# Two small queue changes in a fused long-convolution and state-space kernel: the taps' load on ScalarE's queue, the last stores on SyncE's

## The chip, the cores and the metric

The kernel runs on one core of one Trainium2 chip. The metric is the device time of one execution in microseconds, lower being better. The kernel before took 378.06 us, the median of five runs (377.67 to 381.59).

## The reference, cut to what matters

Two heads work on sequences of 2048 rows and 1024 channels, and their outputs stand side by side in the result.

```python
# head A: a 4-tap convolution, a long convolution by FFT, and a gate
k_shift = sum of k_pad[:, t:t + S, :] * shift_k[:, 3 - t]      # t = 0..3
kv = k_shift * v
y  = irfft(rfft(kv, 2 * S) * rfft(ssm_k, 2 * S))[:S] + kv * ssm_D
a  = q * y
# head B: a diagonal complex recurrence between two projections
Bu = einsum("bld,pd->blp", x, B_bar)
h_t = Lam_bar * h_(t-1) + Bu_t
b  = 2 * real(einsum("blp,dp->bld", h, Cmat)) + x * Dskip
out = concatenate([a, b], axis=-1)
```

`shift_k` holds four taps for each of the 1024 channels, 8 KB in all.

## The kernel before, in words

**Head B** is cut into 16 chunks of 128 time steps. For a chunk, TensorE projects the transposed input (`U`, line 460), ScalarE casts the result out of PSUM (`ue`), VectorE rotates it, scans it along time and rotates it back (`r1`, `r2`, `rc`, `sc`, `r3`, `r4`), TensorE projects to the output (`y_`, lines 529 and 534), ScalarE casts (`ye`, line 545) and a DMA stores the chunk (`yst`, line 553). The last chunk, 15, is stored in two halves directly from `ye` (line 547), because `CFG['th']` names it.

**Head A** is a long convolution written as matrix products, in three stages with scratch tensors in HBM between them. `kvm`, `kv1`, `kv2` and `kva` apply the taps and multiply by v; `am` and `ae` transform, and `ast` (line 627) writes the result to the scratch tensor `Ys_kv`; a parallel path does the same for the filter. The middle stage multiplies spectra. In the last stage, over eight values of u, `a3` transforms back, `a3e` casts into a tile `ot`, `qm` (line 780) multiplies it by q, and `op` (line 786) stores it in four DMAs of 128 KB each.

**Taps.** `ld_w` loads `shift_k` as two rows of 4 KB, one DMA each (line 398). `wb` (line 410) is a matmul of a row of ones with 512 values of such a row, which copies the taps to all 128 partitions; eight of them are needed, the first four reading the second row. `wbe` (line 414) casts each out of PSUM into `wbc`.

**Order.** All of it is written out by hand in one list, `ORDER`, and each engine executes its own instructions in the order of that list. A queue is in order too: an engine that issues a DMA and has to wait for the data holds up everything behind it on that engine. The list begins with `ld_w`. On TensorE the first entries are 22 warm-up products (`wm`), the transposes of one weight block (`bT.6.1`), five more warm-up products, then `wb.4`; on ScalarE the first computing instruction is `bc.6.1` (line 435), a copy of that transposed block. The loads of head B (`bl`, line 429) and of k (`kp`, lines 560 to 562) open SyncE's queue.

The end of the list, with everything but the entries around the stores left out, reads:

```python
... qm.5 ... op.7 ... ye.14.0 ... op.4 ... qp.1 ... ye.14.1 ... op.5 ... qm.0 ... r4.15.1 qm.1 yst.14
y.15.0.2 y.15.0.3 y.15.1.2 ye.15.0 op.0 y.15.1.3 ye.15.1 op.1 yst.15
```

`qp.1` is the last load on SyncE's queue. `yst.15` issues nothing, since chunk 15 is stored by `ye`. Before the change, GpSimd issues every store but those two halves of chunk 15. At the end of the program, line 849 of the launch, the engines drain, and SyncE waits for the outstanding DMAs, before the final signals between engines.

Of the kernel before, what the change touches and what calls it, by code (L numbers as in the profile page):

```python
# [44 lines left out]
    return f(F1), f(F1h), f(G), f(W3)  # L45


CFG = {'kr': 8, 'bdve': 4, 'K4': 13, 'kq': 2, 'tabct': 0, 'swsp': 1, 'th': (15,), 'actsw': ()}

ORDER = """  # L50
ld_w:a0a1 bl.6.1:b0 bl.0.1:b1 kp.-2 ld_G ld_sd ld_F bl.2.1:b2 bl.0.0:b3 wm.22:p0 bT.6.1:p0 wm.5:p1 wb.4:p1 bc.6.1 wb.5:p2 bl.1.0:b4 wb.6:p3 wb.7:p4
# [99 lines left out]
def full_kernel(ctx, tc, A_q, A_k, A_v, A_shift_k, A_ssm_k, A_ssm_D, B_x, B_Lre, B_Lim, B_Bre, B_Bim,  # L151
                B_Cre, B_Cim, B_log_dt, B_Dskip, out, cfg=None):
    c = dict(CFG)
    c.update(cfg or {})
    nc = tc.nc
# [5 lines left out]
    T = 128  # L161
# [6 lines left out]
    out_b = out[0][:, D:2 * D]  # L168
    spd = nc.sync.dma_start
    gpd = nc.gpsimd.dma_start  # L170
# [34 lines left out]
    kr = k.rearrange("(n r s) d -> r n s d", n=32, r=4)  # L205
    vr = v.rearrange("(n r s) d -> r n s d", n=32, r=4)
    qr = q.rearrange("(n r s) d -> r n s d", n=32, r=4)
    oar = out_a.rearrange("(n r s) d -> r n s d", n=32, r=4)
# [9 lines left out]
    st, pools, cms = {}, {}, {}  # L218
# [23 lines left out]
    def k4(name, shape):  # L242
        return rtile(ring, "a", name, shape)
# [143 lines left out]
    def taps_home():  # L387
        if "wbc" not in st:
            a1 = ap_pool("a1")
            st["wbc"] = a1.tile([P, 4, D], BF16, name="wbc", bufs=1)  # L390
            st["kring"] = a1.tile([P, c["kr"], D], BF16, name="kring", bufs=1)
            nc.vector.memset(st["kring"][0:1, 0:4, :], 0.0)

    def ld_w():
        taps_home()
        st["wraw"] = [k4("hk", [P, S]) for _ in range(2)]
        for m in range(2):
            gpd(st["wraw"][m][0:1, :], A_shift_k.rearrange("(o d) j -> o (d j)", o=2)[m:m + 1, :])
    E["ld_w"] = ld_w
    E["ld_F"] = lambda: (gpd(F1t[:], F1d.ap()), gpd(Fht[:].rearrange("p c k -> p (c k)"), Fhd.ap()))  # L400
    E["ld_G"] = lambda: gpd(Gt[:], Gd.ap())
# [148 lines left out]
    def yst(i):  # L550
        yo = st.pop(("yo", i))
        if i not in c["th"]:
            gpd(out_b[i * T:(i + 1) * T, :], yo[:])
    E["yst"] = yst

    def kp(r):
# [225 lines left out]

    def op(u):
        t_ = st.pop(("ot", u))
        for b in range(4):
            gpd(oar[b, :, 2 * u:2 * u + 2, :], t_[32 * b:32 * b + 32, :, :])
    E["op"] = op

    with tc.manual_schedule():
# [64 lines left out]
```

## Time and profile before

| what | value |
|---|---|
| median of five runs | 378.06 us |
| the profiled execution, its own time | 378.51 us |
| its span | 376.6 us |
| TensorE busy | 356.3 us (95%) |
| VectorE busy | 324.8 us (86%) |
| ScalarE busy | 278.3 us (74%) |
| GpSimd busy | 71.7 us (19%) |
| DMA, hardware queue of SyncE | 66.3% of 16 engines' span |
| DMA, software queue of GpSimd | 26.2% |
| line 398, the taps' two DMAs, issue to landing | 4.6 us |
| line 786, stores of `ot`, issue to landing in the last 17 us (median) | 2.7 us |
| line 547, stores of chunk 15, issue to landing | 3.0 us |

The span runs from the first to the last event that the profile records; the 1.9 us that the run's own time has beyond it lies around the program. TensorE is the busiest engine, but a share of the whole says nothing of the first microseconds or the last, and the change touches only these. They have to be read from the timeline, which lists instructions by their start.

### The profile page before, as it was taken

The page shows a single profiled execution, that of the slowest core. Times are in us where ns is not written, and L with a number is a line of the kernel's source. Part 1 is how long each engine was busy: PE and PEld are TensorE (multiplying, and loading weights), DVE is VectorE, ACT ScalarE, POOL GpSimd, SP SyncE. Part 2 cuts the span into 40 slices and gives each one's busy share as a digit, 9 for nine tenths or more (in the row PEclk, how much of TensorE's full clock was granted, in tenths as well). Part 3 has the DMA queues.
Part 4 walks back from the last instruction along what each step waited for, and adds up shares of the span by engine and source line. Part 5 has one row for each costly group of instructions (what it writes and reads, how often), then busy time and mean ns, then how long its engine had stood idle before and what let it go on. Part 6 is the DMA issues. An engine that isn't in the chain of part 4 may idle for free.

```text
span 376.6 us, 9490 instructions
## 1 busy us (share of the span) xinstructions
PE 356.3 (95%) x3821; PEld 248.9 (66%) x3851; DVE 324.8 (86%) x335; ACT 278.3 (74%) x519; POOL 71.7 (19%) x124
## 2 busy tenths in 40 slices
PE   7998698999999999999999999999999999999992
PEld 5787597997577787895865456457764445575640
DVE  2199999998999999999999999459999999159990
ACT  4599979998748876986658996778899975175541
POOL 4000002222431243231000110011010111124541
PEclk9999899999999999999999999999999999999997
DMA  8999999998999887689899899999698999799953
GB/s 192 236 298 245 315 249 276 256 270 238 266 283 223 312 217 223 173 283 327 281 277 265 296 267 297 304 277 354 188 324 219 288 263 332 250 401 401 341 142 95
DMA packets 61642, 101.14 MB, mean 269 GB/s; under 512 B 31535, under 2 KB 33871, under 8 KB 61598
## 3 DMA queue, kind: packets, MB, share of 16 engines
q1 hardware_dynamic: 51502, 67.13, 66.3%
q0 software_dynamic: 10096, 33.40, 26.2%
q8 instruction: 30, 0.49, 0.6%
q14 instruction: 14, 0.11, 0.1%
HBM read 52.27 MB, written 33.55 MB: 228 GB/s over the span
## 4 chain that ended last, share of the span: by engine, by line
PE 68%; ACT 12%; DMA 9%; DVE 4%; issue 3%; SPq 1%; POOL 1%; DVEq 0%; ACTq 0%; POOLq 0%
PE ps_y L529 24%; PE ps_u L460 24%; PE ps_a L692 6%; PE ps_a L732 6%; DMA vv<-Vs 3%; PE ps_a L661 3%; DMA Ys_kv<-ysb 3%; PE ps_y L534 2%; DMA ld<-in_B_B_re_dram 2%; ACT hab L702 2%; ACT ysb L622 1%; ACT x L711 1%; PE ps_a L611 1%; PE ps_t L424 1%; ACT u L462 1%
## 5 line engine op out<-in xcount | busy, mean ns | idle before, releaser
L529 PE MATMUL ps_y<-CT,h 128*128 128x512 bf16 x488 | 122.8, 379 | 2.1 <-DVE h L488 0.8
L460 PEld LDWEIGHTS <-BT 128*128 128x128 bf16 x2048 | 117.5, 98 | 10.2 <-issue 4.7
L460 PE MATMUL ps_u<-xT,BT 128*128 128x128 bf16 x2048 | 122.9, 219 | 1.1 <-DVE BT L435 0.6
L529 PEld LDWEIGHTS <-h 128*128 128x128 bf16 x512 | 45.2, 98 | 47.1 <-issue 1.9
L507 DVE TENSOR_TENSOR_SCAN h<-rtab,h 128x1024 bf16<-128x1024 f32 (+1 forms) x34 | 72.3, 2155 | 0.3
L462 ACT CAST u<-ps_u 128x512 bf16<-128x512 f32 x64 | 40.1, 638 | 29.5 <-PE ps_u L460 28.6
L545 ACT CAST yo<-ps_y 128x512 bf16<-128x512 f32 x32 | 19.5, 613 | 36.0 <-PE ps_y L529 35.7
L723 DVE TENSOR_TENSOR hab<-x,hab 128x2048 bf16<-128x2048 bf16 x32 | 37.9, 1217 | 4.4 <-ACT x L711 3.8
L479 DVE TENSOR_TENSOR mt<-u,Z 128x4096 bf16<-128x4096 bf16 x15 | 34.2, 2287 | 8.0 <-ACT u L462 8.0
L702 ACT CAST hab<-ps_a 128x512 bf16<-128x512 f32 x64 | 36.1, 660 | 4.2 <-PE ps_a L692 2.9
L488 DVE TENSOR_TENSOR h<-mt 128x2048 bf16<-128x2048 bf16 (+1 forms) x34 | 39.0, 1156 | 0.2
L741 ACT CAST vsb<-ps_a 128x512 bf16<-128x512 f32 x64 | 34.9, 646 | 5.7 <-PE ps_a L732 4.7
L711 ACT CAST x<-ps_a 128x512 bf16<-128x512 f32 x64 | 36.6, 677 | 1.5 <-DVE hab L723 0.8
L622 ACT CAST ysb<-ps_a 128x512 bf16<-128x512 f32 x64 | 34.2, 665 | 2.2 <-DMA Ys_kv<-ysb 2.2
L669 ACT CAST ysbh<-ps_a 128x512 bf16<-128x512 f32 x64 | 35.3, 666 | 0.2 <-PE ps_a L661 0.2
L479 DVE TENSOR_TENSOR mt<-h,Z 128x4096 bf16<-128x4096 bf16 x15 | 34.3, 2287 | 0.1
L732 PE MATMUL ps_a<-hab,wts 128*128 128x512 bf16 x122 | 31.2, 379 | 0.2
L582 DVE TENSOR_TENSOR mt<-kring,wbc 128x4096 bf16<-128x4096 bf16 (+3 forms) x16 | 29.9, 1881 | 0.0
L627 POOL DMA_DIRECT2D Ys_kv<-ysb x16 | 11.5, 718 | 91.4 <-ACT ysb L622 91.4
L534 PE MATMUL ps_y<-Dd,xT 128*128 128x128 bf16 x128 | 28.0, 219 | 0.3 <-issue 0.2
L675 POOL DMA_DIRECT2D Ys_h<-ysbh x32 | 22.0, 693 | 30.0 <-ACT ysbh L669 29.2
L745 POOL DMA_DIRECT2D Vs<-vsb x16 | 8.5, 533 | 87.7 <-ACT vsb L741 87.7
(113 smaller groups left out, 404.4 us busy)
## 6 DMA issues: line engine op xcount, KB each, us to landing
Ys_kv<-ysb POOLq DMA_DIRECT2D x16, 512.0 KB, 5.0
Ys_h<-ysbh POOLq DMA_DIRECT2D x32, 256.0 KB, 5.1
l2h<-Ys_h SPq DMA_DIRECT2D x16, 512.0 KB, 4.5
hab<-hab SPq DMA_DIRECT2D x64, 128.0 KB, 4.6
l2k<-Ys_kv SPq DMA_DIRECT2D x16, 512.0 KB, 5.8
Vs<-vsb POOLq DMA_DIRECT2D x16, 512.0 KB, 5.3
vv<-Vs SPq DMA_DIRECT2D x16, 512.0 KB, 11.2
v<-in_A_v_dram SPq DMA_DIRECT2D x32, 128.0 KB, 4.1
```

The source lines that it names most:

```text
L460: nc.tensor.matmul(pu[:, w, jl, :], BT[:, 2 * jp + jl, w, d, :], xT[:, d, :], start=(d == 0), stop=(d == ND - 1))
L462: E["ue"] = lambda i, jp: nc.scalar.copy(st["u", i][:, :, 2 * jp:2 * jp + 2, :], st.pop(("pu", i, jp))[:])
L479: nc.vector.tensor_mul(m4[:].rearrange("p (a b) w -> p a (b w)", a=2), s_, win(Z, h))
L488: nc.vector.tensor_add(dst[:].rearrange("p a j t -> p a (j t)")[:, :, jw], mv[:, :, 0, jw], mv[:, :, 1, jw])
L507: nc.vector.tensor_tensor_scan(gf, rt1[:, jw], gf, 0.0, ALU.mult, ALU.add)
L529: nc.tensor.matmul(py[:], h[:, 1 - w, j, :], CT[:, j, w, dh * 512:(dh + 1) * 512], start=(j == 0 and w == 0), stop=(j == NJ - 1 and w == 1))
L534: nc.tensor.matmul(py[:, dl * P:(dl + 1) * P], st["xT", i][:, d, :], Dd[:, d, :], start=False, stop=False)
L622: nc.scalar.copy(st["ysb", u, rh][:, rl, dh * 512:(dh + 1) * 512], st.pop(("pk", u, dh, r))[:])
L702: nc.scalar.copy(st["hab", g][:, 0, cols], pt[:])
L711: nc.scalar.copy(st["x16", g][:, w * 512:(w + 1) * 512], st.pop(("ps", "l2k", g, w))[:])
L723: nc.vector.tensor_mul(hab[:], st.pop(("x16", g))[:].unsqueeze(1).to_broadcast([P, 2, D]), hab[:])
L732: nc.tensor.matmul(pt[:], st["w", gq][:, gi, 1 + a, :], hab[:, a, w * 512:(w + 1) * 512], start=(a == 0), stop=(a == 1))
```

## The change

The two DMAs of `ld_w` are issued by ScalarE, and four tasks' stores by SyncE instead of GpSimd: `op.5`, `yst.14`, `op.0` and `op.1`, 13 DMAs. `ORDER` is not changed.

```diff
-CFG = {'kr': 8, 'bdve': 4, 'K4': 13, 'kq': 2, 'tabct': 0, 'swsp': 1, 'th': (15,), 'actsw': ()}
+CFG = {'kr': 8, 'bdve': 4, 'K4': 13, 'kq': 2, 'tabct': 0, 'swsp': 1, 'ldw': 1, 'th': (15,), 'actsw': (), 'late': (('op', 5), ('yst', 14), ('op', 0), ('op', 1))}
...
-            gpd(st["wraw"][m][0:1, :], A_shift_k.rearrange("(o d) j -> o (d j)", o=2)[m:m + 1, :])
+            (nc.scalar.dma_start if c["ldw"] else gpd)(st["wraw"][m][0:1, :], A_shift_k.rearrange("(o d) j -> o (d j)", o=2)[m:m + 1, :])
...
-            gpd(out_b[i * T:(i + 1) * T, :], yo[:])
+            (spd if ("yst", i) in c["late"] else gpd)(out_b[i * T:(i + 1) * T, :], yo[:])
...
+        f = spd if ("op", u) in c["late"] else gpd
         for b in range(4):
-            gpd(oar[b, :, 2 * u:2 * u + 2, :], t_[32 * b:32 * b + 32, :, :])
+            f(oar[b, :, 2 * u:2 * u + 2, :], t_[32 * b:32 * b + 32, :, :])
```

`spd` is `nc.sync.dma_start` and `gpd` is `nc.gpsimd.dma_start`.

## The prediction

> **What bounds the kernel now.** I read the list of waits of TensorE first, then the timeline of the first 60 us and of the last 25, and last what the closing line of the program executes.
>
> The waits of TensorE over the whole span (who waited for whom: us in total, times, longest):
>
> ```profile
> PE ps_a L611 <- DVE acc L600: 2.1, 1, 2.1
> PE ps_a L410 <- DMA hk<-in_A_shift_k_dram: 1.4, 1, 1.4
> PE ps_t L424 <- ACT ysb L622: 1.2, 1, 1.2
> ...
> PE ps_t L424 <- DMA ld<-in_B_B_im_dram: 1.0, 1, 1.0
> PE ps_a L661 <- ACT ysb L622: 0.8, 1, 0.8
> PE ps_y L529 <- DVE h L488: 0.8, 1, 0.8
> ```
>
> There are few, and by their windows all but the last fall before 60 us, the last at 360. Between, TensorE is busy some 19.8 of every 20 us: what starts that stretch earlier ends it earlier. One of the early waits is for the taps. The timeline (start, duration, engine, line, operation; in brackets the idle time before it and who ended it):
>
> ```profile
> 0.74 1.28 ACT L435 ACT_TABLE_LOAD   x1 [0.74 <-PEq L838]
> ...
> 1.52 1.16 POOL L398 DMA_DIRECT2D hk<-in_A_shift_k_dram  x2
> ...
> 4.86 1.01 ACT L435 COPY BT<-ps_t 128x1024 bf16<-128x1024 bf16 x1 [2.83 <-PE ps_t L424]
> ...
> 6.80 1.88 PE L410 MATMUL ps_a<-hk,ones 1*128 1x512 bf16 x4 [1.45 <-DMA hk<-in_A_shift_k_dram]
> ```
>
> GpSimd issues the taps at 1.52 us, after its constants; TensorE is free for them at 5.36 and gets them at 6.80. Later in the same stage stand a long store and what waits for it:
>
> ```profile
> 46.76 0.74 POOL L627 DMA_DIRECT2D Ys_kv<-ysb  x1 [41.93 <-ACT ysb L622]
> ...
> 57.30 2.05 ACT L622 CAST ysb<-ps_a 128x512 bf16<-128x512 f32 x4 [2.22 <-DMA Ys_kv<-ysb]
> ```
>
> The end, by the same view, and then all that the closing line runs (engine, operation, count: shortest/median/longest ns, first and last start):
>
> ```profile
> 365.41 3.13 PEld L529 LDWEIGHTS <-h 128*128 128x128 bf16 x16 [0.37 <-DVE h L488]
> 366.78 2.13 POOL L786 DMA_DIRECT2D out_dram<-ot  x4 [0.63 <-DVE ot L780]
> 367.35 0.59 ACT L545 CAST yo<-ps_y 128x512 bf16<-128x512 f32 x1 [3.35 <-PE ps_y L529]
> 367.96 2.09 SPq L547 DMA_DIRECT2D out_dram<-yo  x2
> 369.07 0.59 ACT L545 CAST yo<-ps_y 128x512 bf16<-128x512 f32 x1 [1.14 <-PE ps_y L529]
> ```
>
> ```profile
> L849 POOLq DRAIN  x3: 46/99/7627, 368.1 to 376.3; - x3
> L849 SPq DRAIN  x3: 7/7/7, 372.8 to 376.0; - x3
> ```
>
> Computation is over at 369.66, SyncE has seen its last store land by 372.8 (369.7 + 3.0), and yet the span ends at 376.6. GpSimd's first drain starts at 368.1 and takes 7.63 us, to 375.73; all other closing events follow within 0.87 us. **GpSimd's drain bounds the end**, not a landing.
>
> **What the Trainium skill says.** (1) "DMA: Bandwidth & Descriptors", Specifications: first-byte latency about 1 us on GpSimd's software path, about 0.6 us from SyncE or ScalarE. The trace has no load on ScalarE's queue; its issues take 0.50 to 0.65 us on GpSimd and 0.33 to 0.43 on SyncE, the same direction. (2) The same page, Issuing engines are not separate DMA queues: all share the same 16 DMA engines. The trace can't contradict it; so the taps still compete with SyncE's first loads. (3) "ScalarE: Activation LUTs", What ACT_TABLE_LOAD costs: 1283 ns for the load; the trace has 1.28 us. (4) "VectorE: DVE Perf Modes", The DRAIN you can't avoid: boilerplate drains of program ends are constant, about 12 ns. SyncE's 7 ns agrees; GpSimd's 7627 ns does not, and the measurement decides.
>
> **The taps, step by step.** Removed from GpSimd: two issues, 1.16 us. Its four constants behind them (`Gt`, `sd`, `F1t`, `Fht`) move up by as much; nobody waits for them. Added on ScalarE: two issues. Nearest row: SyncE's first loads, 0.40 and 0.42 us, so from 0.75 to about 1.6. Queued behind them on ScalarE is the table load, then 1.6 to 2.9, and then the first copy at 4.86: 2 us of cover, cost nothing. (Were the cover gone, it would be 0.85 us.) `wb.4` reads the second row, issued at about 1.2. With the 3.0 us that SyncE's first load takes from issue to its transpose (0.75 to 3.78) it lands at 4.2; with the taps' own 4.6, at 5.8. TensorE's wait shrinks from 1.45 to between 0 and 0.4. I take 1.4 us gained at this place. The other bound: ScalarE's issues could hold up SyncE's first two by up to 0.4 us each, a loss of 0.8.
>
> What becomes of the 1.4: the list goes on without slack to the parameter transpose at 18.02 (its data was issued by 9.4), VectorE's table chain, ScalarE's row without gaps from 24 to 46, and the store at 46.76. Loads on this way landed with about that much to spare: the block transposed at 31.78 is late already (1.0 us wait), but ScalarE comes to it only some 2 us after that transpose. So `Ys_kv` is issued up to 1.4 earlier. It took 10.45 us in a crowded stage (median of its kind 5.0), ScalarE stood idle 2.22 us for it, and TensorE 0.83 behind that. If the landing moves with the issue, all 1.4 passes through; if the DMA backlog fixes it at 57.22, nothing does. Bounds 0 and 1.4; I take **0.9**, nearer to the issue since two queues share the engines. After 60 us nothing absorbs it.
>
> **The stores, step by step.** GpSimd loses 13 issues of about 0.54 us; its last is now `op.4`'s, ended at about 357. If its drain still takes 7.6 us, it is over at 365, beside computation, and no longer on the path. SyncE gains 13 issues, at 0.42 each with a 0.04 gap (its row of the q loads has 0.31 to 0.42). No load is behind them: `qp.1` was the last, over at 353.4. `op.5` (ready 355.4) and `yst.14` (360.1) pass while SyncE would otherwise wait. Then SyncE waits for `ye.15.0` until 367.94, and with it `op.0`, ready since 363.5, and `op.1`, ready at 366.5: this wait is the change's new one, and only the end waits for it. The sum: half of chunk 15 at 367.96; `op.0` from 368.37, four times 0.46, to 370.21; the other half, ready at 369.68, to 370.6, so 0.5 us late; `op.1` at 370.62, the last of its four starting at 372.0. Landing: the stores of chunk 15 took 3.0 us, so 375.0; at 2.7 us and issues of 0.31 us it is 374.0; at 4.6 (median of line 786 over the span) it is 376.6. What decides now is that landing against 375.73: a gain of **0.7**, bounds +1.7 and -0.9. SyncE seems to have some eight DMAs in flight at most (q loads at one per 1 us with landings of 7.6); then the third and fourth of `op.1` wait for landings of about 371, which is before their turn. If these are late, up to 1 us more is lost.
>
> The sum is 0.9 + 0.7 = 1.6 us. The profiled execution took 378.51 (span 376.6 and 1.9 around it), 0.45 above the median; it would become 376.9 with a span of 375.0, and the median 378.06 becomes **376.5**.
>
> **The rivals.** *Tail only:* the taps' gain ends in the `Ys_kv` landing, or the taps land no earlier, because SyncE's first loads fill the engines (DMA share 1.0 from 2 us on), so that this part does not do what it says. For it: ScalarE's idle 2.22 us at that landing. Against: two queues share. Time 378.06 - 0.7 = 377.4. *SyncE becomes the end:* ten stores in one row behind the wait for `ye.15.0`. It decides once the last landing is more than 3.7 us after the last start at 372.0 (375.73); at 4.6 it costs 0.9, with waits for earlier landings 1.9, so 379.0 to 380.0 where the start gives nothing. For it: a median landing of 4.6 over the span. Against: 2.7 to 3.0 in the last stage, where little else moves. *A new late load:* with TensorE earlier, or ScalarE's issues among SyncE's, some load misses its turn after 60 us and a wait of a few us opens, as at `Ys_kv`; slower, 382. Against: no DMA wait of TensorE after 60 in this trace. *More than counted:* stage boundaries between 40 and 58 us fall better, the Ys_kv landing shortens towards its median; down to 373.5.
>
> **How the numbers follow.** The forecast 0.55, tail only 0.20, SyncE as the end 0.15, late load 0.05, more than counted 0.05. The range reaches from both gains at their bounds (1.4 + 1.5, 375.2) to SyncE as the end at 0.9 with nothing from the start (379.0); it leaves out the far cases. One per cent is 3.8 us, about what a measurement of this kernel can tell from no change; no case but the last two gets there: faster 0.05, same 0.89, slower 0.06.
>
> **What would show it.** In the changed profile: the taps on ScalarE's queue before the table load, TensorE's 1.45 us at line 410 nearly gone, the parameter transpose near 16.6, `Ys_kv` issued near 45.4, ScalarE's wait for it longer or not; GpSimd's long drain starting near 357; SyncE's waits for landings ending near 375 and only 0.9 us left after it. Wrong if GpSimd's drain lasts to the end all the same, if SyncE's issues are slower than 0.46 us, or if TensorE waits for a DMA after 60 us.

## The result, and the profile after

The kernel after the change took 375.75 us (median of 43 runs, 373.32 to 378.4) against 377.11 us for the kernel before (80 runs, 372.92 to 381.59). The ratio is 0.9969, with a 95% interval of 0.9955 to 0.9982: 1.2 us faster, 0.7 to 1.7. The two medians themselves differ by 1.4 us. The forecast was 1.6 us from a median of 378.06, so 376.5.

Single executions of one kernel differ by more than the effect (from 373 to 378 us after the change), and so do profiles. The profiled execution after has a span of 372.8 us against 376.6, a difference of 3.8 us that must not be read as the change's worth. Below, the span is split at the end of the last cast (line 545): what comes before is the **front**, what comes after is the **tail**. The tail turns out to repeat within 0.1 us from profile to profile of one kernel, while the front varies by up to 3 us. A diff line adds one to the line numbers behind it: line 786 is now 787, and 849 is 850.

The taps, in the timeline after (start, duration, engine, line, operation):

```profile
0.74 0.76 ACTq L398 DMA_DIRECT2D hk<-in_A_shift_k_dram  x2
...
1.53 1.28 ACT L435 ACT_TABLE_LOAD   x1 [1.53 <-PEq L839]
...
5.41 1.86 PE L410 MATMUL ps_a<-hk,ones 1*128 1x512 bf16 x4
```

The two issues take 0.76 us together, the table load follows at 1.53, and TensorE comes to the taps at 5.41 with no wait. What it waits for now (us in total, times, longest):

```profile
PE ps_t L424 <- ACT ysb L622: 1.7, 1, 1.7
PE ps_t L424 <- DMA ld<-in_B_B_im_dram: 1.3, 1, 1.3
...
PE ps_t L424 <- DMA ld<-in_B_C_im_dram: 0.9, 2, 0.6
PE ps_t L424 <- DMA ld<-in_B_C_re_dram: 0.8, 1, 0.8
PE ps_y L529 <- DVE h L488: 0.8, 1, 0.8
PE ps_t L424 <- DMA ld<-in_B_B_re_dram: 0.5, 1, 0.5
```

The line of the taps is gone. In its place stand waits of the transposes for their own loads: 1.3 + 0.9 + 0.8 + 0.5 = 3.5 us, of which the kernel before had 1.0. On the other side, the longest wait of the kernel before, 2.1 us at line 611 for VectorE's `acc`, is down to 0.2. TensorE reaches the blocks earlier than they land; how much of the gain is given back there, this list alone doesn't say. The store of `Ys_kv` and its waiter:

```profile
44.54 0.73 POOL L627 DMA_DIRECT2D Ys_kv<-ysb  x1 [40.76 <-ACT ysb L622]
```

```profile
53.87 2.05 ACT L622 CAST ysb<-ps_a 128x512 bf16<-128x512 f32 x4 [0.25 <-DMA Ys_kv<-ysb]
```

It is issued 2.2 us earlier than in the first profile and lands 9.3 us after its issue, where it took 10.45 before; ScalarE waits 0.25 us instead of 2.22. The landing moved with the issue, and moved more than it. The taps can account for 1.45 of the 2.2 us at most; the rest goes with TensorE's earlier full rate in this profile (last section).

The end in the timeline after, and the drains of the closing line (count: shortest/median/longest ns, first and last start):

```profile
364.09 0.59 ACT L545 CAST yo<-ps_y 128x512 bf16<-128x512 f32 x1 [3.34 <-PE ps_y L529]
364.70 0.36 SPq L547 DMA_DIRECT2D out_dram<-yo  x1
365.15 1.81 SPq L787 DMA_DIRECT2D out_dram<-ot  x4
365.81 0.59 ACT L545 CAST yo<-ps_y 128x512 bf16<-128x512 f32 x1 [1.14 <-PE ps_y L529]
367.06 0.38 SPq L547 DMA_DIRECT2D out_dram<-yo  x1
367.54 1.83 SPq L787 DMA_DIRECT2D out_dram<-ot  x4
```

```profile
L850 POOLq DRAIN  x3: 46/108/6709, 353.2 to 372.5; - x3
L850 SPq DRAIN  x3: 7/7/7, 372.0 to 372.3; - x3
```

GpSimd's long drain starts at 353.2 and is over before 360, beside computation. The row of ten stores on SyncE is what the forecast laid out: half of chunk 15, four, the other half, four. SyncE comes to its drain at 372.0, and 0.8 us later the span ends. The tail is 372.8 - 366.4 = 6.4 us, against 376.6 - 369.66 = 6.9 before.

### The profile page after: what moved, and what is told of

Its sections match the earlier page's. It is cut to its first block, busy times and chain, and to the rows that moved or that the text cites. A ratio compares the mean times of both kernels' runs of the same rounds, so it can differ in the third digit from the quotient of the medians.

```text
span 372.8 us, 9487 instructions
## 1 busy us (share of the span) xinstructions
PE 355.1 (95%) x3821; PEld 247.9 (67%) x3851; DVE 324.6 (87%) x335; ACT 278.3 (75%) x519; POOL 63.7 (17%) x109
## 4 chain that ended last, share of the span: by engine, by line
PE 74%; DMA 11%; ACT 8%; DVE 2%; issue 2%; SPq 1%; DVEq 0%; ACTq 0%
PE ps_u L460 28%; PE ps_y L529 25%; PE ps_a L692 6%; PE ps_a L732 6%; DMA ld<-in_B_B_im_dram 4%; PE ps_a L661 4%; DMA vv<-Vs 3%; DMA ld<-in_B_C_re_dram 2%; PE ps_y L534 2%; PE ps_t L641 2%; DMA ld<-in_B_B_re_dram 2%; ACT hab L702 2%; ACT x L711 1%; PE ps_a L611 1%; PE ps_t L424 1%
```

## The experiments

All are compared with the kernel before, run between them on the same chip. The ratio and its interval are worked out from the single runs and are not the quotient of the two medians: `stores_first_2` is 3.0 us below before by its ratio and 3.9 by the medians. The front is the median less the profile's tail, and the last column compares it with the front of the kernel before in the same row (tail 6.9). It is worked out from medians of 6 to 80 runs and one tail each, so a few tenths mean nothing.

| kernel | taps on | median us | before us | ratio, 95% interval | tail us | front against before |
|---|---|---|---|---|---|---|
| whole change | ScalarE | 375.75 | 377.11 | 0.9969 (0.9955 to 0.9982) | 6.4 | -0.9 |
| taps_only | ScalarE | 375.59 | 376.61 | 0.9972 (0.9954 to 0.9990) | 6.9 | -1.0 |
| one_on_pool | ScalarE | 375.12 | 376.61 | 0.9963 (0.9944 to 0.9982) | 6.9 | -1.5 |
| stores_first | ScalarE | 372.75 | 376.61 | 0.9907 (0.9878 to 0.9936) | 3.6 | -0.5 |
| stores_first_2 | ScalarE | 372.47 | 376.35 | 0.9921 (0.9889 to 0.9954) | 3.6 | -0.6 |
| stores_first_taps_sp | SyncE | 372.58 | 376.35 | 0.9914 (0.9881 to 0.9947) | 3.6 | -0.4 |
| stores_only | GpSimd | 375.53 | 376.61 | 0.9966 (0.9948 to 0.9984) | 5.7 | +0.1 |
| stores_first_taps_pool | GpSimd | 372.26 | 376.55 | 0.9885 (0.9846 to 0.9924) | 2.8 | -0.2 |
| stores_first_taps_pool_2 | GpSimd | 372.26 | 376.35 | 0.9893 (0.9852 to 0.9933) | 2.8 | 0.0 |
| gap_filled | GpSimd | 376.34 | 376.55 | 0.9985 (0.9966 to 1.0003) | 6.9 | -0.2 |
| taps_late | GpSimd, later | 380.08 | 376.55 | 1.0092 (1.0066 to 1.0117) | 6.9 | +3.5 |

### One half alone

`taps_only`, against the whole change, as are all edits below unless said otherwise (`...` stands for what is left out of a line):

```diff
-... 'late': (('op', 5), ('yst', 14), ('op', 0), ('op', 1))}
+... 'late': ()}
```

> Only the taps' load is moved to ScalarE; all stores stay on GpSimd as before. Tail means the time from the end of the last cast (line 545) to the end of the span: 6.9 us before, 6.4 after the whole change. Theory (two separate gains that add): TensorE's 1.45 us wait at line 410 is gone, tail 6.9 again, time 0.9 us below before (bounds 0 and 1.4). Rival 1 (all of the gain is at the start): 1.2 to 1.4 below before. Rival 2 (the gain at the start ends in the Ys_kv landing): 0.0 to 0.3 below before, and ScalarE waits some 3.6 us for that landing.

Measured 1.0 us below before (0.4 to 1.7), with no wait at line 410 and the tail of before. The middle of the interval lies with the theory; rival 1 is not excluded by it, rival 2 lies just outside: ScalarE did not wait for the `Ys_kv` landing at all in this profile.

`stores_only`:

```diff
-... 'ldw': 1, ...
+... 'ldw': 0, ...
```

> Only the last stores are moved to SyncE; the taps stay on GpSimd. Theory: the taps' wait of 1.45 us is back, tail 6.4, time 0.5 us below before. Rival 1 (start only): same as before within 0.2. Rival 2 (end only): 1.2 below before.

Measured 1.3 us below before (0.6 to 2.0), with a wait of 1.49 us at line 410. Rival 1 falls. The theory's 0.5 us lies just outside the interval, and the 1.2 of rival 2 in its middle. Rival 2 has the right time for another reason: the tail is 5.7 and not the expected 6.4, so that the tail alone brings 1.2 us. The two halves add up to 2.3 us where the whole brought 1.2. The intervals would allow that as chance; the tails, which repeat, do not look like chance, and are taken up below.

### The drain

`one_on_pool`:

```diff
-... 'late': (('op', 5), ('yst', 14), ('op', 0), ('op', 1))}
+... 'late': (('op', 5), ('yst', 14), ('op', 0))}
```

> The whole change, but the four stores of op.1 stay on GpSimd. Theory (GpSimd's drain takes 6 to 7 us from its last DMA issue, however few DMAs came before): the long drain is at the end again, tail 6.9, time 0.5 us above the whole change. Rival (the drain works off what the software queue still has to do, so four DMAs need less): tail 5 to 5.5, time up to 1 us below the whole change.

The timeline of GpSimd and the drains of the closing line in this kernel:

```profile
363.51 2.13 POOL L787 DMA_DIRECT2D out_dram<-ot  x4 [9.93 <-DVE ot L780]
```

```profile
L850 POOLq DRAIN  x3: 46/99/7312, 364.9 to 372.7; - x3
L850 SPq DRAIN  x3: 7/7/125, 370.8 to 372.4; - x3
```

With four DMAs after ten idle microseconds the drain is nearly as long as with a full queue: its end is 6.5 us after the end of the last issue, where it was 6.9 in the kernel before and 6.1 in the kernel after. The tail is 6.9 again, while SyncE had seen its last landing at 370.6. So the theory holds for the tail, and the rival's 5 to 5.5 us fall. (What the drain waits for is taken up in the last section: it is not a fixed time from the issue.) Its time doesn't show the half microsecond: at 375.12 it lies 0.6 below the median of the whole change, which was measured at another time; that is inside what such medians differ by.

### The row on SyncE

`stores_first` moves two words of the order list ahead:

```diff
-... y.15.0.2 y.15.0.3 y.15.1.2 ye.15.0:b4 op.0 y.15.1.3 ye.15.1 op.1 yst.15
+... op.0 op.1 y.15.0.2 y.15.0.3 y.15.1.2 ye.15.0:b4 y.15.1.3 ye.15.1 yst.15
```

> The whole change, and in the order list op.0 and op.1 stand ahead of chunk 15's last products, so that SyncE issues these eight stores before it waits for chunk 15's casts. Theory (after the change the end is SyncE's row of stores behind that wait): the last store is chunk 15's second half, issued as soon as its cast is over, tail 0.4 + 3.0 landing + 0.9 = about 4.1 us instead of 6.4, time 2.3 us below the whole change and 3.5 below before. Rival (the closing events or the landing of a crowded row set the end, not the row's order): tail 6 or more, time within 0.4 of the whole change.

SyncE's last issues in the timeline, and the drains:

```profile
360.59 4.74 SPq L787 DMA_DIRECT2D out_dram<-ot  x8
365.43 1.68 SPq L547 DMA_DIRECT2D out_dram<-yo  x2
```

```profile
L850 POOLq DRAIN  x3: 46/99/6748, 353.7 to 370.0; - x3
L850 SPq DRAIN  x3: 7/7/7, 369.5 to 369.8; - x3
```

The eight stores go out while TensorE still multiplies, the last cast ends at 366.73, and its store is issued at 366.75. The tail falls to 3.6 us (0.5 below the expected 4.1, since the landing took 1.9 us and not 3.0) and the time to 372.75, 3.5 below before. The rival falls: after the change it is the order of SyncE's row that set the end. This version beats both kernels.

### What the taps' place is worth

> The kernel before, but GpSimd issues the taps after its four constants instead of ahead of them, some 2.2 us later. Theory (what the taps' landing holds up at line 410 passes through to the end in good part): TensorE's wait grows from 1.45 to about 3.6 us, time 1.4 us above before (bounds 0.7 and 2.2). Rival (the first 60 us have slack, the landing of Ys_kv or the loads set the pace): within 0.4 of before.

```diff
-ld_w:a0a1 bl.6.1:b0 bl.0.1:b1 kp.-2 ld_G ld_sd ld_F ...
+bl.6.1:b0 bl.0.1:b1 kp.-2 ld_G ld_sd ld_F ld_w:a0a1 ...
```

This edit is against the kernel before. The taps are issued at 3.80, and the timeline of TensorE shows

```profile
10.43 1.88 PE L410 MATMUL ps_a<-hk,ones 1*128 1x512 bf16 x4 [5.07 <-DMA hk<-in_A_shift_k_dram]
```

a wait of 5.07 us instead of 1.45: the DMA itself took 6.1 us now, probably because it met the loads in full flow. The time rose by 3.5 us (2.5 to 4.4) for 3.6 us of wait. A delay here passes through nearly or entirely, and the rival falls; the expectation had the size of the wait wrong, and with it the time. So a delay at this place is on the path; what becomes of a *gain* is another question, since loads can be late for an engine that comes early.

`gap_filled`, also against the kernel before, lets TensorE work until the taps come, to separate the delay from the idle time:

```diff
-... bT.6.1:p0 wm.5:p1 wb.4:p1 ...
+... bT.6.1:p0 wm.15:p1 wb.4:p1 ...
```

> The kernel before, with ten more warm-up products ahead of the first taps' product, so that TensorE is busy while it would wait for the taps and comes to them at the same time. Theory (the taps' landing holds up what follows): same as before within 0.4. Rival (not the delay but the idle time matters, because TensorE comes to its full rate later after a gap): 0.7 to 1.2 below before, and the transposes at line 424 go from 1.0 to 0.6 us for eight some 3 us earlier than in the profile of before (there between 16.6 and 18.6).

It stays with before, as the theory has it (0.6 us below, interval 1.3 below to 0.1 above), but that interval doesn't exclude the rival. And a wait of 1.26 us remained, because TensorE came to its full rate just then in this execution and went through the fifteen products in 1.0 us. The transposes went to 0.6 us between 13.5 and 14.8 us, some 3 us before the first profile of before, yet not before the second (told below). The test is weak and leaves open whether idle time has a part of its own.

`stores_first_taps_pool`, twice, and `stores_first_taps_sp` vary the queue of the taps in the kernel with the short tail (the order of `stores_first` stays):

```diff
# stores_first_taps_pool
-... 'ldw': 1, ...
+... 'ldw': 0, ...
# stores_first_taps_sp
-            (nc.scalar.dma_start if c["ldw"] else gpd)(st["wraw"][m][0:1, :], ...
+            spd(st["wraw"][m][0:1, :], ...
```

> The kernel with op.0 and op.1 ahead of chunk 15's last products, with the taps on GpSimd again: beside the run of stores_first it shows what the taps alone are worth. Theory: tail 3.6 us again, time 0.9 us above stores_first (372.75), so 2.6 below before. Rival (the taps are worth nothing): as stores_first, 3.5 below before.

> stores_first once more, so that the three places for the taps' load can be compared on one chip with a short tail. Theory: 3.5 us below before; 0.9 below the same kernel with the taps on GpSimd. Rival (the taps are worth nothing): as the same kernel with the taps on GpSimd, within 0.3.

> The same with the taps on GpSimd. Theory: a wait of 1.0 to 1.8 us at line 410, 0.9 us above stores_first_2. Rival (the taps are worth nothing): within 0.3 of it.

> The same with the taps at the head of SyncE's queue. Theory (what counts is when line 410 can run, not the queue): no wait at line 410, but the first block of B is issued 0.8 us later and its transposes start at 4.6 instead of 3.81, so line 410 at 6.2: time between the two others, 0.3 to 0.8 us above stores_first_2. Rival (only the taps' landing counts): as stores_first_2 within 0.3.

Here the expectation failed: with the taps on GpSimd again the kernel is no slower (372.26 both times against 372.75 and 372.47), and its tail is not the 3.6 us that were expected. By the time alone the rival wins, and the taps' load would be worth nothing. The tails say what stands against it: 2.8 us twice with the taps on GpSimd, 3.6 three times with the taps on ScalarE or SyncE. The tail takes back 0.8. Whether the front gains anything here is not shown: it is 0.4 us shorter by the medians of the four kernels with the taps on ScalarE or GpSimd, 0.2 by their means, and with 6 to 8 runs each such a difference is known to about 1 us either way. On SyncE line 410 ran at 5.77 us instead of 5.41, since the first block of B was issued 0.7 us later; its time is not told apart from the two others, so the expected 0.3 to 0.8 us above `stores_first_2` is not confirmed.

### Where the 0.8 us of the tail come from

Before SyncE's first drain stand nine waits in one fixed order. Eight of them name the semaphores on which DMAs of the hardware queues report (a semaphore is the counter by which a DMA tells that it has landed); the first of the nine is for GpSimd's. These DMAs take the eight in turn, so two DMAs more on the hardware queues shift the last store to another of them. This is SyncE's end of program in two kernels, as the trace records it (us from the start; the semaphore waited for):

```
whole change: last store reports on 102, landed 371.11
369.42 S116  370.74 S100  371.13 S102  371.20 S104  371.27 S105
371.67 S106  371.76 S107  371.82 S108  371.89 S118  371.96 drain
stores_only: last store reports on 118, landed 370.48
368.74 S114  368.81 S101  368.88 S103  369.28 S104  369.37 S105
369.43 S106  369.74 S116  370.06 S117  370.49 S118  370.56 drain
```

In the whole change the last landing is the third wait, and six more follow it, 0.85 us until the drain, though their data had landed before. In `stores_only` it is the ninth, and 0.08 us follow. The same holds in every profile here in which SyncE's stores set the end: third place and 0.82 to 0.85 us in the five with the taps on a hardware queue, ninth and 0.08 in the three with the taps on GpSimd. The list of SyncE's waits at the end shows the other side of it, first for `stores_first`, then for `stores_first_taps_pool`: SyncE sits 0.8 us less in waits for landings, because it has gone through the other waits before.

```profile
SPq L850 <- DMA out_dram<-yo: 1.4, 2, 0.9
```

```profile
SPq L850 <- DMA out_dram<-yo: 0.6, 1, 0.6
```

The last store landed 1.87 us after its issue in both; what differs is what SyncE still had to do behind it. With `taps_only` and `one_on_pool` the turn doesn't matter, since GpSimd's drain ends later anyway. That the order of the waits is the cause is read from the rows of waits in eight profiles, where it accounts for the 0.75 us between the tails to within 0.05; a kernel that shifts the turn by two and leaves all else alone was not tried.

### Two more profiles

> The kernel before, once more, for a second profile. Theory (the time at which TensorE comes to its full rate at the start varies from run to run): the parameter transpose (line 264), at 18.0 us in the first profile and at 15.2 to 16.6 in the others, falls at another time, anywhere from 16.5 to 18.5, with the same 1.45 us wait at line 410 and the tail of 6.9 us. Rival (late taps fix it at 18.0): 17.8 to 18.2.

The transpose of the parameters, at 18.02 us in the first profile, stands at 16.27 in the second, with a tail of 6.9. The rival falls, and the time lies a little below the expected 16.5. The wait at line 410 is 1.03 us and not the expected 1.45: in the profiles with the taps first on GpSimd's queue it lies between 1.0 and 1.75. The front is 2.9 us shorter (366.80 against 369.66). So the first profile of before was a late one.

> The whole change, once more, for a second profile of its tail. Theory (the tail is SyncE's row of stores plus one landing, and landings vary by about 1 us from run to run): no wait at line 410, tail between 5.5 and 6.5 us, no wait of a few us of TensorE after 60 us. Rival (the tail of 6.4 is fixed by something else than the landing): 6.3 to 6.5.

No wait at line 410, and a tail of 6.4 us again: the rival is right, the landings (2.18 and 2.20 us) do not vary by a microsecond. This is what made the tails worth comparing at all.

## Why the prediction was right

**The sum and its direction.** 1.6 us were forecast, 1.2 measured (0.7 to 1.7); 375.75 lies in the range. The base of the forecast, the median of five runs, was 0.95 above the median of eighty. Two small slips of the forecast bear on nothing: its range takes 1.5 us for the stores where the bound was 1.7, and GpSimd's issues do not end at 0.65 us, as the line of the store at 46.76 with its 0.74 shows.

**The taps.** The wait at line 410 went from 1.45 us to nothing, by the mechanism and the queue order that were forecast; the table load waited behind the issues and nothing waited for it (the first copy starts at 4.85 us, 4.86 before). Of the 1.45 us the forecast let 0.9 through. The fronts with the taps on ScalarE are 0.5 to 1.5 us shorter than before, 0.9 on average over five, and those with the taps on GpSimd unchanged within 0.2. That both say 0.9 is partly luck: the forecast chose it between bounds of 0 and 1.4, and its account of the way there is not confirmed. The loss was put at the `Ys_kv` landing. There it shows in the second profile of the kernel after, with 2.2 us of TensorE behind ScalarE's cast at line 622, and not in the first. Instead, TensorE waits longer for head B's loads, 2.6 us on average in the seven profiles with the taps on a hardware queue against 1.05 in the six with the taps first on GpSimd's, and less for VectorE at line 611, 1.15 against 2.1. Single profiles cross this line: `stores_only`, with the taps on GpSimd, waits 3.1 us for these loads. How the gain reaches the end is therefore open. The rival *tail only*, that the start gives nothing, falls narrowly by `taps_only`, whose gain of 0.4 to 1.7 us comes with the tail of before; with the short tail neither it nor the theory is shown.

**The stores.** GpSimd's drain left the path, as forecast, and a single task's stores put it back. The row of issues on SyncE came out to 0.2 us: its last issue starts 2.5 us after the last cast, where the forecast had 372.0 - 369.66 = 2.3. Two terms behind it were mis-sized and cancel, which is luck: the landing was taken at 3.0 us, from stores that ran beside GpSimd's, and was 2.2; and nothing was counted between landing and drain, where 0.85 us of waits lie. The gain is 0.5 us instead of 0.7. The rival *SyncE becomes the end* named the right place, since SyncE's row does set the end now; but the loss that it feared needs a landing of more than 3.7 us.

**What was missed.** The two parts were summed as if they could not touch each other. By the row of waits they do: moving the taps to a hardware queue costs 0.8 us in the row of closing waits as soon as SyncE's stores set the end. In halves the change would be 1.0 in the front and 1.2 in the tail (6.9 - 5.7); together 2.2 less 0.7 (6.4 - 5.7), so 1.5, beside 1.4 by the two medians and 1.2 by the ratio. And a step that the forecast laid out itself, `op.0` and `op.1` ready since 363.5 and 366.5 and queued behind a wait until 367.94, was priced and left there; taking it away is worth 2.8 us of tail, more than the whole change.

## What to carry to other kernels

Look at what the closing line of the program executes before costing an end: here the last engine to drain, and not the last landing, set the end, and it was GpSimd, whose queue the profile lists as a software queue. When stores are gathered on one in-order queue, put those whose data is ready ahead of the one that waits for the last result. When executions differ by more than the effect, split the span where the work changes hands: one part may repeat to a tenth of a microsecond and show what the medians hide.

## What the runs showed of the hardware that was not expected

GpSimd's first drain at the end of the program ended 6.0 to 6.9 us after the end of its last DMA issue in all fourteen profiles. That is not one fixed time. In the eight profiles with no store of the last ten microseconds on GpSimd, the time from the issue varies from 6.0 to 6.8 us, but the drain ends 2.91 us after the last store of its queue has landed, in each of them. There it behaves like a wait for that landing with 2.9 us behind it. In the five with all the last stores but chunk 15's halves on GpSimd, it took 7.62 to 7.64 us each time and ended 3.6 to 4.0 us after the last landing; `one_on_pool` lies between, with 3.1. What sets the end in these is open. The Trainium skill ("VectorE: DVE Perf Modes", The DRAIN you can't avoid) gives about 12 ns for the drains around a program; SyncE's 7 ns agree, GpSimd's first drain does not.

One source of the front's variation is that TensorE comes to its full rate at another time in each execution. The same eight transposes take 1.01 us at first and 0.61 later; in the second profile of before they change between 12.6 and 14.0 us, in the first between 15.8 and 18.6, and in the first profile of the kernel after between 13 and 14. In the profile of `taps_only` the rate came early and was lost again:

```profile
3.81 1.01 PE L424 MATMUL ps_t<-ident,ld 128*128 128x128 bf16 x8
...
6.36 0.62 PE L424 MATMUL ps_t<-ident,ld 128*128 128x128 bf16 x8
...
9.88 1.04 PE L424 MATMUL ps_t<-ident,ld 128*128 128x128 bf16 x8 [1.10 <-DMA ld<-in_B_B_im_dram]
```

The Trainium skill ("TensorE: Matmul & The Clock Gate", Part 1: The HAM clock gate) describes two rates and a free-running window of activity that decides between them, whose phase a kernel doesn't set; these profiles agree in that the moment moves while the program is the same. The clock column does not show the first, slow stretch: it reads 1.00 up to 17 us in the first profile of before, while eight transposes take 1.01 us. So the rate there is to be read from the durations.

The full rate can also be lost a second time. In the first profile of before:

```profile
42.09 1.01 PE L424 MATMUL ps_t<-ident,ld 128*128 128x128 bf16 x8 [1.18 <-ACT ysb L622]
...
46.48 0.61 PE L424 MATMUL ps_t<-ident,ld 128*128 128x128 bf16 x8
```

This time the clock column shows it, with 0.83 between 40 and 50 us, where the second profile of the kernel after has 1.00. Such a stretch at half the clock, 3.4 or 6.8 us long and beginning between 37 and 42 us, stands in five of the six profiles with the taps first on GpSimd's queue and in three of the seven with the taps on a hardware queue. It begins during or soon after the waits around line 611, which are longer in the first group. This is a second source of the front's variation, and a way in which the taps' place may reach the end; it was read from the profiles and not tested.
